# Cross-attention, gated MLP and squared-ReLU MLP on one core: other places for early loads, weight stores and attention steps

## The chip, the core and the metric

One core of one Trainium2 chip runs the whole program in one launch. The metric is the device time of one execution in microseconds (us); the kernel before takes 1464.22 us, the median of three runs (1463.28 to 1471.02).

## What is computed

The reference is three layers, one after the other. Inputs are x (8 batches, 8 heads, 512 tokens, 64 values) and state (8, 8, 32, 64), float32; the MLP weights are float64.

```
scores  = x @ state^T / 8        a  = softmax(scores)    xread = a  @ state
scores2 = state @ x^T / 8        a2 = softmax(scores2)   sread = a2 @ x
t = concat(xread, sread) as (8 * 544 tokens, 512)
t = (sigmoid(t @ w_gate) * (t @ w_val)) @ w_out          # d_ff = 1536
t = relu(t @ w_in)^2 @ w_out2                            # d_ff = 2048
```

The result has 4352 x 512 float32 values.

## The kernel before

Every product is three TensorE matmuls: each float32 operand is split into a high and a low part, and `mm3` (lines 182 to 185) adds high x high, high x low and low x high in PSUM. So nearly all matmul rows carry one of the lines L183, L184, L185. A float64 weight block is first made float32 by `to_single` (lines 109 to 134: two ScalarE passes L116 and L118, four VectorE ones L119, L123, L127, L131) and then split (L138 on ScalarE, L139 on VectorE).

Since `a @ state` is followed at once by `@ w_gate` and `@ w_val`, the kernel multiplies the states by the weights first. The 1536 columns are six **chunks** of 256 gate and 256 value columns. `chunk_steps` loads the four weight blocks of a chunk, converts them (`conv_gv`), multiplies them with the states of four batches (`state_weights`, PSUM tile `ps_g`, copied out by L531 and L535 into `go`), and stores the products in DRAM (`store_g`, L543, tensors `gd`). The two `w_out` blocks of the chunk are converted on the way. The chunks run once for batches 0 to 3 and once for batches 4 to 7; for the second pass the converted weights are read back from `wd` in DRAM, where `state_weights` (L525) or `store_kept` (L511) has put them. Six weight blocks (`KEPT`) lie in buffers that are free until later output weights need them, so their store can wait; the others lie in a pool of two buffers (`wr_p`).

Attention of a batch has steps in two halves (`group_stages`): token-major x is loaded (`xtok`), transposed on TensorE (L318) and split (L324, L325), multiplied with a block-diagonal state (`ps_s`, L337), and goes through transpose, maximum, subtraction, exponential, sum, reciprocal, product and transpose on VectorE and ScalarE (L347 to L370) into the tile `a`. There is one block-diagonal tile, filled by GpSimd (`prep_diag`), and one buffer each for most temporaries. The softmax in the other direction comes much later; its token-major x is loaded by `load_xn` into one buffer.

A **unit** is one batch and 128 of the 1536 columns. Its front (`front_x`) loads the products `gd` of its batch and chunk into `gi` (L597), splits them into `gg` (L607 on ScalarE, L608 on GpSimd), multiplies them with `a` into `psg` and `psv`, takes the sigmoid of `psg` (L622), the product with `psv` (L630, VectorE) and splits it (L190, L191). Its back (`back1`) multiplies with `w_out` into four accumulators `acc`. There are twelve units for a batch. The first four batches run their units 0 to 5, then all four their units 6 to 11; the accumulators of a first segment are stored (`pd`) and added later.

Order: `spread` gives every step of chunks and attentions a place in units, and the units call these steps in turn. On top of this a scheduler sets the final order of each engine from its own estimate of times. Unless `issue_after` ties an instruction to another, it may move a load far ahead. `reads` is the list of the units' `gi` loads, and `behind(reads)` ties to its last one.

All loads and stores named here are issued by SyncE (SP) in order; an issue whose buffer is not free holds everything behind it.

Of the kernel before, what the change touches and what calls it, by code (L numbers as in the profile page):

```python
# [18 lines left out]
P = 128  # L19
# [3 lines left out]
QB = 4  # L23
# [9 lines left out]
def kernel(  # L33
# [12 lines left out]
    nc = tc.nc  # L46
    B, H, S, D = x.shape
    NS = state.shape[2]
# [4 lines left out]
    NF1 = DF1 // P  # L53
# [7 lines left out]
    BM = B // NM  # L61
# [33 lines left out]
    def helper(busy):  # L95

        return nc.gpsimd if busy else nc.vector
# [38 lines left out]
    def convert(raw, w, busy):  # L136
        cf = to_single(raw, busy)
        nc.scalar.copy(out=w[:, 0, :], in_=cf)  # L138
        helper(busy).tensor_sub(out=w[:, 1, :], in0=cf, in1=w[:, 0, :].bitcast(F32))  # L139
# [3 lines left out]
    def row_src(w, f):  # L143
        return [(every, w.bitcast(U32)[f * P : (f + 1) * P, :])]
# [16 lines left out]
    def width(b):  # L161
# [6 lines left out]
    w_dram = {  # L168
        (ch, c): dram.tile([P, 2, 512], F32, name=f"wd{ch}_{c}")
        for ch in range(NCH) for c in range(NPAIR)  # L170
    }
# [10 lines left out]
    def mm3(ps, lh, ll, rh, rl, start, stop, more=False):  # L182
        nc.tensor.matmul(ps, lh, rh, start=start, stop=False, skip_group_check=more)  # L183
        nc.tensor.matmul(ps, lh, rl, start=False, stop=False, skip_group_check=more)  # L184
        nc.tensor.matmul(ps, ll, rh, start=False, stop=stop, skip_group_check=more)  # L185
# [21 lines left out]
    diag = once_p.tile([P, 2, NPAIR, P], F32R, name="diag")  # L207
    nc.gpsimd.memset(diag.bitcast(U32), 0)

    def load_states(m):  # L210
        raw = f_p.tile([P, DM], F32, tag="xs", name="sraw", bufs=1)
        for i in range(BM):
            nc.sync.dma_start(
                out=raw[NS * i : NS * (i + 1)].rearrange("n (h d) -> n h d", h=H),
                in_=state[BM * m + i].rearrange("h n d -> n h d"),
            )
        return raw

    def prep_states(raw):
# [26 lines left out]
    by_pair = x.rearrange("b (g j k) s d -> b g j k s d", g=2, j=2)  # L246
# [24 lines left out]
    def load_xn(b, g):  # L271

        t = xn_p.tile([P, 2, 2 * NT, D], F32, tag="xn", name="xn")
        for j in range(2):
            nc.sync.dma_start(
                out=t[:, j],
                in_=by_pair[b, g, j].rearrange("c (t p) d -> p (c t) d", p=P),
            )
        loaded_xn[b, g] = t

    a_tiles = {}
# [213 lines left out]
    gv = {}  # L495
    g_out = {}

    reads, sigs = [], []

    def behind(done):  # L500
        return tc.issue_after(done[-1].ins) if done else nullcontext()

    KEPT = {key: NF1 // 2 + i for i, key in enumerate(
        ((1, 0), (1, 1), (1, 2), (1, 3), (2, 0), (2, 1))
    )}
    kept = []

    def store_kept(after):
# [4 lines left out]
    def conv_gv(ch, c, raw):  # L513
        if (ch, c) in KEPT:
            f = KEPT[ch, c]
            w1[f] = gv[ch, c] = w1_p.tile([P, 2, 512], F32R, name=f"o{f}")
            kept.append((w1[f], w_dram[ch, c]))
        else:
            gv[ch, c] = wr_p.tile([P, 2, 512], F32R, tag="w", name="w")
        convert(raw, gv[ch, c], False)  # L520

    def state_weights(ch, c, m):
        w = gv.pop((ch, c))
        if m == (ch < ONCE) and (m or (ch, c) not in KEPT):
            nc.sync.dma_start(out=w_dram[ch, c], in_=w.bitcast(F32))  # L525
        ps = [at_p.tile([P, 512], F32, tag="at", name="ps_g") for j in range(2)]
        for j in range(2):
            sh, sl = (st_t[:, i, c, j, :] for i in range(2))
            mm3(ps[j], sh, sl, w[:, 0, :], w[:, 1, :], True, True)
        o = go_p.tile([P, 2, 512], F32, tag="go", name="go")  # L530
        nc.scalar.copy(out=o[:, 0, :], in_=ps[0])  # L531
        if m:
            nc.vector.tensor_copy(o[:, 1, :], ps[1])
        else:
            nc.scalar.copy(out=o[:, 1, :], in_=ps[1])  # L535
        g_out[ch, c, m] = o
# [8 lines left out]
    def conv_out1(f, raw):  # L545
        if f not in w1:
            w1[f] = w1_p.tile([P, 2, 512], F32R, name=f"o{f}")
        convert(raw, w1[f], False)

    ONCE, PACED = 1, (3,)  # L550

    def chunk_steps(ch, m, outs):

        raws = {}
        jobs = [("p", c) for c in range(NPAIR)] + [("o", f) for f in outs]
        steps = []
        ready = m and ch >= ONCE

        def load(n):
            k, i = jobs[n]  # L560
            if ready:
                gv[ch, i] = raw_p.tile([P, 2, 512], F32R, tag="raw", name="wagain")
                nc.sync.dma_start(out=gv[ch, i].bitcast(F32), in_=w_dram[ch, i])
                return
            with behind(reads if ch in PACED and not m else ()):
                raws[n] = load_pair(ch, i) if k == "p" else load_raw(row_src(w_out1, i))

        def conv(n):
            k, i = jobs[n]
            with behind(sigs if ch in PACED and not m else ()):  # L570
                if k == "p":
                    conv_gv(ch, i, raws.pop(n))
                else:
                    conv_out1(i, raws.pop(n))

        steps += [lambda: load(0), lambda: load(1)]
        for n in range(len(jobs) + 2):
            if n < len(jobs):
                if not ready:
                    steps.append(lambda n=n: conv(n))  # L580
                if not ready and n + 2 < len(jobs):
                    steps.append(lambda n=n: load(n + 2))
            if 1 <= n <= NPAIR:
                steps.append(lambda n=n: state_weights(ch, n - 1, m))
                if ready and n + 1 < len(jobs):
                    steps.append(lambda n=n: load(n + 1))
            if 2 <= n <= NPAIR + 1:
                steps.append(lambda n=n: store_g(ch, n - 2, m))
        return steps
# [628 lines left out]
        hl = st["g"]  # L1218
        squared("s", ps.rearrange("p i n -> p (i n)"), raw=True, into=(hl[:, 0], hl[:, 1]))

    HALF = NF1 // 2
    segments = [(b, 0, HALF) for b in range(QB)] + [(b, HALF, NF1) for b in range(QB)]
    segments += [(b, 0, NF1) for b in range(QB, B + 1)]
    units = [(b, f, lo, hi - 1) for b, lo, hi in segments for f in range(lo, hi)]
    at_unit = {(b, f): i for i, (b, f, _, _) in enumerate(units)}
# [4 lines left out]
    def spread(fns, start, end):  # L1230

        for i, fn in enumerate(fns):
            queue.append((STEPS * (start + (end - start) * i / max(len(fns), 1)), len(queue), fn))
# [6 lines left out]
    raw = load_states(0)  # L1240
    att_a, att_b = {}, {}
# [18 lines left out]

    outs = {ch: list(range(FC * ch, FC * (ch + 1))) for ch in range(NCH)}
    spread(chunk_steps(1, 0, outs[1]), 0, 1)
    spread(chunk_steps(2, 0, outs[2]), 1.2, 3)
    spread(att_a[1], 1, 4)
    spread(att_a[2], 4, 8)
    spread(att_a[3], 8, 12)
    for ch in range(3, NCH):
        spread(chunk_steps(ch, 0, outs[ch]), 6 + 4.5 * (ch - 3), 10.5 + 4.5 * (ch - 3))
    second = []
    spread([lambda: second.append(load_states(1))], 21.5, 21.5)  # L1270
    spread([lambda: prep_states(second.pop())], 23.5, 23.5)
# [27 lines left out]
    for i, (b, f, lo, hi) in enumerate(units):  # L1299
        ch, ff = divmod(f, FC)  # L1300
# [20 lines left out]
    for i, (b, f, lo, hi) in enumerate(units):  # L1321
        count[0] = STEPS * i
        g = (front_x if b < B else front_s)(b, f)
# [97 lines left out]
```

## Time and profile before

| what | value |
|---|---|
| median of three runs | 1464.22 us |
| the profiled execution's own time | 1464.19 us |
| its span, first to last instruction | 1462.4 us |
| mean granted TensorE clock | 0.988 |
| TensorE busy | 1408.3 us, 96% |
| VectorE busy | 1029.2 us, 70% |
| ScalarE busy | 903.5 us, 62% |

The span is 1.8 us shorter than the execution's own time, and that time is 0.03 us from the median. Shares of the whole span hide that the start is another regime: in the first 50 us TensorE is busy for 30.30 us, between 200 and 250 us for all 50.

### The profile page before, as it was taken

How to read it: one execution, taken by the hardware profiler on the slowest of the kernel's cores; microseconds unless marked ns; L12 is line 12 of the kernel's file. 1: busy time of each engine (PE TensorE's matmuls, PEld its weight loads, DVE VectorE, ACT ScalarE, POOL GpSimd, SP SyncE). 2: the span in 40 equal slices, each digit the busy share in tenths (PEclk: the TensorE clock that was granted, in tenths of full speed). 3: DMA queues.
4: the chain of work that ended last, by engine and by line, in shares of the span. 5: the costliest groups of instructions: out<-in, count | busy, mean ns of one | idle time of the engine just before them, and what ended most of it. 6: DMA issues, size and time to landing. Idle time of an engine off the chain costs nothing.

```text
span 1462.4 us, 21778 instructions
## 1 busy us (share of the span) xinstructions
PE 1408.3 (96%) x7416; PEld 1201.1 (82%) x7416; DVE 1029.2 (70%) x1644; ACT 903.5 (62%) x1630; POOL 303.5 (21%) x280
## 2 busy tenths in 40 slices
PE   5889999999999899999999999999999999999998
PEld 3568788887777687888897888799989999988898
DVE  6969887578788878777426756756787578745665
ACT  6869786466668867675427744655667456655432
POOL 1112213223334443445004443100000000000000
PEclk9899999999999999999999999999999999999999
DMA  9879899799998573564858965765667566866765
GB/s 257 260 236 322 230 305 328 222 337 322 329 310 252 166 186 112 158 211 153 305 195 311 333 220 192 236 221 191 194 218 262 182 196 197 272 228 216 234 228 173
DMA packets 293119, 347.50 MB, mean 238 GB/s; under 512 B 108048, under 2 KB 204816, under 8 KB 293008
## 3 DMA queue, kind: packets, MB, share of 16 engines
q1 hardware_dynamic: 288112, 336.93, 71.7%
q0 software_dynamic: 2048, 7.34, 1.4%
q10 hardware_dynamic: 2848, 1.84, 0.4%
q8 instruction: 59, 0.97, 0.3%
q14 instruction: 52, 0.43, 0.1%
HBM read 248.51 MB, written 97.52 MB: 237 GB/s over the span
## 4 chain that ended last, share of the span: by engine, by line
PE 71%; DMA 9%; DVE 7%; ACT 6%; issue 3%; POOL 2%; SPq 1%; ACTq 0%; POOLq 0%; DVEq 0%
PE o L185 7%; PE o L183 7%; PE o L184 7%; PE acc L184 4%; PE acc L185 4%; PE acc L183 4%; PE px L183 3%; PE px L184 3%; PE px L185 3%; PE psg L183 3%; PE psv L183 2%; PE psg L184 2%; PE psg L185 2%; PE psv L184 2%; PE psv L185 2%
## 5 line engine op out<-in xcount | busy, mean ns | idle before, releaser
L608 POOL TENSOR_TENSOR gg<-gi,gg 128x512 fp32r<-128x512 f32 x96 | 132.6, 1382 | 311.7 <-ACT gg L607 281.3
L183 PE MATMUL o<-wp,gh 128*128 128x256 f32 x672 | 188.9, 283 | 1.9 <-DMA wp<-wt 1.8
L184 PE MATMUL o<-wp,gh 128*128 128x256 f32 x672 | 188.9, 283 | 0.0
L185 PE MATMUL o<-wp,gl 128*128 128x256 f32 x672 | 185.5, 283 | 0.0
L184 PE MATMUL acc<-gl,o 128*128 128x512 f32 (+1 forms) x432 | 163.4, 381 | 3.0 <-DVE gl L191 3.0
L185 PE MATMUL acc<-gh,o 128*128 128x512 f32 (+1 forms) x432 | 162.5, 379 | 0.0
L183 PE MATMUL acc<-gh,o 128*128 128x512 f32 (+1 forms) x432 | 137.4, 380 | 0.4 <-DVE yp L694 0.4
L183 PEld LDWEIGHTS o<-wp,gh 128*128 128x128 f32 x672 | 128.4, 191 | 5.6 <-ACT gh L1062 1.8
L184 PEld LDWEIGHTS o<-wp,gh 128*128 128x128 f32 x672 | 128.5, 191 | 2.6
L185 PEld LDWEIGHTS o<-wp,gl 128*128 128x128 f32 x672 | 126.6, 191 | 1.2
L1123 DVE TENSOR_TENSOR y<-o,y 128x512 f32<-128x512 f32 x144 | 97.0, 685 | 34.7 <-PE o L185 33.8
L191 DVE TENSOR_TENSOR gl<-g,gh 128x512 fp32r<-128x512 f32 (+1 forms) x108 | 86.0, 797 | 28.7 <-ACT gh L190 28.3
L183 PE MATMUL px<-xh,wi 128*128 128x512 f32 x256 | 100.8, 395 | 3.4 <-DVE c L1013 2.4
L184 PE MATMUL px<-xl,wi 128*128 128x512 f32 x256 | 100.6, 393 | 0.0
L185 PE MATMUL px<-xh,wi 128*128 128x512 f32 x256 | 99.8, 390 | 0.0
L184 PEld LDWEIGHTS acc<-gl,o 128*128 128x128 f32 x432 | 81.3, 188 | 20.3 <-DVE gl L191 6.0
L185 PEld LDWEIGHTS acc<-gh,o 128*128 128x128 f32 x432 | 81.4, 188 | 14.8
L183 PEld LDWEIGHTS acc<-gh,o 128*128 128x128 f32 x432 | 79.2, 188 | 16.3 <-ACT c L118 0.8
L190 ACT CAST gh<-g 128x512 fp32r<-128x512 f32 (+1 forms) x108 | 64.4, 596 | 44.7 <-DVE g L630 31.3
L183 PE MATMUL psg<-a,gg 128*128 128x512 f32 x192 | 77.6, 404 | 9.9 <-ACT sg L622 6.4
L630 DVE TENSOR_TENSOR g<-psv,sg 128x512 f32<-128x512 f32 x96 | 65.4, 681 | 30.3 <-PE psv L185 21.0
L1053 ACT ACTIVATE c<-c 128x512 f32<-128x512 f32 x72 | 45.4, 631 | 65.5 <-DVE c L1013 64.8
(222 smaller groups left out, 3820.8 us busy)
## 6 DMA issues: line engine op xcount, KB each, us to landing
wi<-wi SPq DMA_DIRECT2D x256, 256.0 KB, 3.8
gd<-go SPq DMA_DIRECT2D x192, 128.0 KB, 4.2
gi<-gd SPq DMA_DIRECT2D x96, 256.0 KB, 4.1
wp<-wt SPq DMA_DIRECT2D x96, 256.0 KB, 3.5
wp<-wo SPq DMA_DIRECT2D x72, 256.0 KB, 3.5
wi<-wa SPq DMA_DIRECT2D x32, 512.0 KB, 4.6
wo<-wo SPq DMA_DIRECT2D x32, 512.0 KB, 4.8
ws<-wd SPq DMA_DIRECT2D x24, 512.0 KB, 5.8
```

Of the source, the lines that this page charges most:

```text
L183: nc.tensor.matmul(ps, lh, rh, start=start, stop=False, skip_group_check=more)
L184: nc.tensor.matmul(ps, lh, rl, start=False, stop=False, skip_group_check=more)
L185: nc.tensor.matmul(ps, ll, rh, start=False, stop=stop, skip_group_check=more)
L190: nc.scalar.copy(out=gh[:, :n], in_=g32[:, :n])
L191: nc.vector.tensor_sub(out=gl[:, :n], in0=g32[:, :n], in1=gh[:, :n].bitcast(F32))
L608: nc.gpsimd.tensor_sub(out=t[:, 1], in0=src, in1=t[:, 0].bitcast(F32))
L630: nc.vector.tensor_mul(out=g32, in0=ps, in1=sg)
L1053: nc.scalar.activation(out=r, in_=c, func=AF.Relu)
L1123: nc.vector.tensor_add(out=y, in0=ps[to, j], in1=y)
```

## The change

Five things differ. `load_states` and `load_xn` are tied behind the first `gi` load: for the states of batches 4 to 7 and for the first `xn` this decides; the first state load has no read to wait for and stays. Two more weight blocks, (2, 2) and (2, 3), are stored behind a `gi` load, ahead of the six kept ones; they lie in the pool of two buffers. The first segments of batches 0 and 1 have four units and not six, so the order of units is batch 0 (0 to 3), batch 1 (0 to 3), batch 2 (0 to 5), batch 3 (0 to 5), and then the rest. Chunk 2 is spread over units 2 to 5 (it was 1.2 to 3), the attentions of batches 1, 2, 3 over 1 to 2.6, 2.6 to 5, 5 to 8.5 (they were 1 to 4, 4 to 8, 8 to 12), and the chunks from the third on over 4.2 units each from 8 (they were 4.5 each from 6).

```diff
     def load_states(m):
         raw = f_p.tile([P, DM], F32, tag="xs", name="sraw", bufs=1)
         for i in range(BM):
-            nc.sync.dma_start(
+            with behind(reads[:1]):
+                nc.sync.dma_start(
...
         for j in range(2):
-            nc.sync.dma_start(
-                out=t[:, j],
+            with behind(reads[:1]):
+                nc.sync.dma_start(
+                    out=t[:, j],
...
+    LAST = ((2, 2), (2, 3))
...
             gv[ch, c] = wr_p.tile([P, 2, 512], F32R, tag="w", name="w")
+            if (ch, c) in LAST:
+                kept.insert(LAST.index((ch, c)), (gv[ch, c], w_dram[ch, c]))
...
-        if m == (ch < ONCE) and (m or (ch, c) not in KEPT):
+        if m == (ch < ONCE) and (m or (ch, c) not in (*KEPT, *LAST)):
...
-    HALF = NF1 // 2
-    segments = [(b, 0, HALF) for b in range(QB)] + [(b, HALF, NF1) for b in range(QB)]
+    FIRST = (4, 4, 6, 6)
+    segments = [(b, 0, FIRST[b]) for b in range(QB)] + [(b, FIRST[b], NF1) for b in range(QB)]
...
-    spread(chunk_steps(2, 0, outs[2]), 1.2, 3)
-    spread(att_a[1], 1, 4)
+    spread(chunk_steps(2, 0, outs[2]), 2, 5)
+    spread(att_a[1], 1, 2.6)
```

The names in the order: `xn` is token-major x for the later softmax, `sraw` the raw states, `raw` a float64 weight block; `gd_2_124` is the product of chunk 2 for batch 0, `gd_0_128` that of chunk 0 for batch 1. On SyncE, at the very start, before:

```order
L156 DMA raw<-in_moe_w_val_dram 128x2x256
L275 DMA xn<-in_x_dram 128x8x64 x2
L213 DMA sraw<-in_state_dram 32x8x64 x4
L156 DMA raw<-in_moe_w_gate_dram 128x2x256
L156 DMA raw<-in_moe_w_val_dram 128x2x256
L106 DMA raw<-in_moe_w_out_dram 128x1024
```

On SyncE, at the first unit's read, now:

```order
L602 DMA gi<-gd_0_122 128x2x256 x2
L219 DMA sraw<-in_state_dram 32x8x64
L548 DMA gd_1_123<-go 32x2x512
L548 DMA gd_1_129<-go 32x2x512
L548 DMA gd_1_135<-go 32x2x512
L548 DMA gd_1_141<-go 32x2x512
L156 DMA raw<-in_moe_w_gate_dram 128x2x256
```

The six issues have left the first weight loads and stand between the stores of chunk 1 and the loads of chunk 2 (the other three `sraw` and the two `xn` follow a dozen rows on). On SyncE, the read of the fifth unit, before (batch 0, chunk 2):

```order
L348 DMA sd_0_196<-s_900 128x512
L543 DMA gd_2_124<-go 32x2x512
L543 DMA gd_2_130<-go 32x2x512
L543 DMA gd_2_136<-go 32x2x512
L543 DMA gd_2_142<-go 32x2x512
L597 DMA gi<-gd_2_124 128x2x256 x2
```

and now (batch 1, chunk 0):

```order
L355 DMA sd_0_196<-s_781 128x512
L271 DMA xtok<-in_x_dram 128x8x64 x2
L602 DMA gi<-gd_0_128 128x2x256
L355 DMA sd_1_197<-s_851 128x512
L602 DMA gi<-gd_0_128 128x2x256
L514 DMA wd_2_180<-w 128x1024
L548 DMA gd_2_124<-go 32x2x512
```

The fifth unit now reads a product that was stored long ago, and the store of chunk 2 comes behind it. On ScalarE, the products of chunk 3 (`go` copies), before, among the sigmoids of several units:

```order
L622 ACTIVATE sg<-psg 128x512
L531 COPY go<-ps_g 128x512
L116 ACTIVATE q<-raw 128x512
L535 COPY go<-ps_g 128x512
L351 ACT_TABLE_LOAD
L351 ACTIVATE e_1383<-e_1383 128x512
L607 CAST gg<-gi 128x512
L138 CAST w<-c 128x512
L190 CAST gh<-g_1516 128x512
```

and now, the last of a block that lies between the sigmoids of the fourteenth and the fifteenth unit:

```order
L138 CAST w<-c 128x512
L536 COPY go<-ps_g 128x512
L138 CAST o_540<-c 128x512
L116 ACTIVATE q<-raw 128x512
L540 COPY go<-ps_g 128x512
L376 CAST a<-a_1436 128x512
L118 ACTIVATE c<-raw 128x512
L536 COPY go<-ps_g 128x512
L118 ACTIVATE c<-raw 128x512
L540 COPY go<-ps_g 128x512
L627 ACT_TABLE_LOAD
L627 ACTIVATE sg<-psg 128x512
```

All eight `go` copies of chunk 3 now stand between two sigmoids, together with the last part of the attention of batch 3.

## Rows read from the trace of the kernel before

**Rows 1.** First line of the page: busy time, share, instructions.

```profile
PE 1408.3 (96%) x7416; PEld 1201.1 (82%) x7416; DVE 1029.2 (70%) x1644; ACT 903.5 (62%) x1630; POOL 303.5 (21%) x280
```

**Rows 2.** Stretches: length, busy PE, PEld, DVE, ACT, POOL, clock, DMA share, GB/s.

```profile
0.00:50.00 50.00, 30.30 (x80) 19.06 (x81) 38.24 (x78) 36.19 (x63) 9.06 (x18) 0.83 1.00 276
70.00:80.00 10.00, 10.00 (x49) 8.31 (x48) 9.22 (x18) 7.34 (x14) 0.00 (x0) 1.00 0.65 196
80.00:90.00 10.00, 7.81 (x36) 5.43 (x34) 4.34 (x8) 5.81 (x9) 1.16 (x4) 1.00 0.55 148
90.00:100.00 10.00, 8.11 (x28) 6.43 (x29) 7.04 (x12) 5.96 (x8) 2.52 (x2) 0.66 1.01 333
200.00:250.00 50.00, 50.00 (x222) 40.85 (x221) 39.57 (x66) 35.20 (x64) 14.78 (x13) 1.00 0.97 332
```

**Rows 3.** Timeline of ScalarE: sigmoids of units 4, 5, 6, 10, 14, 22.

```profile
73.37 0.59 ACT L622 ACTIVATE sg<-psg 128x512 f32<-128x512 f32 x1
...
95.70 0.60 ACT L622 ACTIVATE sg<-psg 128x512 f32<-128x512 f32 x1 [1.15 <-PE psg L185]
...
102.05 0.60 ACT L622 ACTIVATE sg<-psg 128x512 f32<-128x512 f32 x1
...
126.18 0.59 ACT L622 ACTIVATE sg<-psg 128x512 f32<-128x512 f32 x1
...
158.21 0.58 ACT L622 ACTIVATE sg<-psg 128x512 f32<-128x512 f32 x1
...
214.65 0.60 ACT L622 ACTIVATE sg<-psg 128x512 f32<-128x512 f32 x1
```

**Rows 4.** Timeline of TensorE: the fifth unit's start, and a dense stretch.

```profile
91.89 0.79 PE L183 MATMUL psg<-a,gg 128*128 128x512 f32 x1 [3.28 <-ACT gg L607]
...
92.90 0.63 PE L183 MATMUL psv<-a,gg 128*128 128x512 f32 x1
93.33 0.63 PE L184 MATMUL psv<-a,gg 128*128 128x512 f32 x1
...
209.79 0.39 PE L183 MATMUL psg<-a,gg 128*128 128x512 f32 x1
...
211.61 0.39 PE L185 MATMUL psv<-a,gg 128*128 128x512 f32 x1
```

**Rows 5.** Chain that ended last, the piece ahead of the fifth unit.

```profile
88.38 2.76 DMA gi<-gd
```

**Rows 6.** Timeline of VectorE around the fourth unit's product.

```profile
70.16 0.42 DVE L119 TENSOR_SCALAR c<-c 128x512 f32<-128x512 f32 x1
70.49 0.69 DVE L131 CUSTOM_DVE_ANT_0 c<-c,q 128x1024 uint16<-128x1024 uint16 x1
...
74.77 0.68 DVE L630 TENSOR_TENSOR g<-psv,sg 128x512 f32<-128x512 f32 x1
75.37 0.68 DVE L139 TENSOR_TENSOR o<-c,o 128x512 fp32r<-128x512 f32 x1
```

**Rows 7.** Timeline of ScalarE: an operation after a sigmoid, and a table load.

```profile
73.86 0.61 ACT L138 CAST o<-c 128x512 fp32r<-128x512 f32 x1
...
100.75 1.28 ACT L622 ACT_TABLE_LOAD   x1
```

**Rows 8.** Timeline of SyncE, at the start.

```profile
7.16 1.49 SPq L275 DMA_DIRECT2D xn<-in_x_dram  x2
8.77 3.93 SPq L213 DMA_DIRECT2D sraw<-in_state_dram  x4
12.80 0.39 SPq L156 DMA_DIRECT2D raw<-in_moe_w_gate_dram  x1
```

**Rows 9.** Waits of the first 60 us: total, times, longest.

```profile
DVE q L127 <- DMA raw<-in_moe_w_val_dram: 8.5, 1, 8.5
```

**Rows 10.** Timelines of GpSimd and VectorE at one moment.

```profile
63.27 2.83 POOL L608 TENSOR_TENSOR gg<-gi,gg 128x512 fp32r<-128x512 f32 x2 [12.07 <-ACT gg L607]
...
63.43 1.52 DVE L119 TENSOR_SCALAR c<-c 128x512 f32<-128x512 f32 x1
```

More of the change, by code (lines that the diff above doesn't have):

```diff
@@ L208, with behind @@
     nc.gpsimd.memset(diag.bitcast(U32), 0)
+    reads, sigs = [], []
+    def behind(done):
+        return tc.issue_after(done[-1].ins) if done else nullcontext()
     def load_states(m):
@@ L212, in load_states @@
         for i in range(BM):
-            nc.sync.dma_start(
-                out=raw[NS * i : NS * (i + 1)].rearrange("n (h d) -> n h d", h=H),
-                in_=state[BM * m + i].rearrange("h n d -> n h d"),
-            )
+            with behind(reads[:1]):
+                nc.sync.dma_start(
+                    out=raw[NS * i : NS * (i + 1)].rearrange("n (h d) -> n h d", h=H),
+                    in_=state[BM * m + i].rearrange("h n d -> n h d"),
+                )
         return raw
@@ L274, in load_xn @@
         for j in range(2):
-            nc.sync.dma_start(
-                out=t[:, j],
-                in_=by_pair[b, g, j].rearrange("c (t p) d -> p (c t) d", p=P),
-            )
+            with behind(reads[:1]):
+                nc.sync.dma_start(
+                    out=t[:, j],
+                    in_=by_pair[b, g, j].rearrange("c (t p) d -> p (c t) d", p=P),
+                )
         loaded_xn[b, g] = t
@@ L496 @@
     g_out = {}
-    reads, sigs = [], []
-    def behind(done):
-        return tc.issue_after(done[-1].ins) if done else nullcontext()
     KEPT = {key: NF1 // 2 + i for i, key in enumerate(
@@ L1262 @@
     spread(chunk_steps(1, 0, outs[1]), 0, 1)
-    spread(chunk_steps(2, 0, outs[2]), 1.2, 3)
-    spread(att_a[1], 1, 4)
-    spread(att_a[2], 4, 8)
-    spread(att_a[3], 8, 12)
+    spread(chunk_steps(2, 0, outs[2]), 2, 5)
+    spread(att_a[1], 1, 2.6)
+    spread(att_a[2], 2.6, 5)
+    spread(att_a[3], 5, 8.5)
     for ch in range(3, NCH):
-        spread(chunk_steps(ch, 0, outs[ch]), 6 + 4.5 * (ch - 3), 10.5 + 4.5 * (ch - 3))
+        spread(chunk_steps(ch, 0, outs[ch]), 8 + 4.2 * (ch - 3), 12.2 + 4.2 * (ch - 3))
     second = []
```

## The prediction

> **What bounds the kernel now.** I read the page first. TensorE is busy for 1408.3 of 1462.4 us [rows 1], so at most 54 us of idle time can go, and the question is where it lies. The stretches answer that: TensorE has 30.30 busy us in the first 50, and from 200 to 250 us all 50 [rows 2]. The change reorders work ahead of the 22nd unit and hardly behind it, so only the first 215 us count.
>
> A busy TensorE can be a slow one, so I measured lateness. In a dense stretch matmuls start 0.2275 us apart (the last of rows 4 starts 1.82 us and eight matmuls behind the one above it); between 92 and 97 us they start 0.43 us apart, and the granted clock of 90 to 100 us is 0.66, so this is partly the lower of the two clock levels [rows 2, 4]. I counted, in the order, the 512-wide matmuls up to the last `psg` of a unit (four transposes as one), took 0.2275 us for each, and subtracted that from the time of the unit's sigmoid [rows 3]. What is left is the time that TensorE has lost so far:
>
> - unit 4: 73.37 - 140 x 0.2275 = 41.5
> - unit 5: 95.70 - 208 x 0.2275 = 48.4
> - unit 6: 102.05 - 218 x 0.2275 = 52.5
> - unit 10: 126.18 - 323 x 0.2275 = 52.7
> - unit 14: 158.21 - 456 x 0.2275 = 54.5
> - unit 22: 214.65 - 690 x 0.2275 = 57.7
>
> So 41.5 us are lost before the fourth unit, where weights are converted; 11.0 between the fourth and the sixth; 5.2 in small pieces up to the 22nd. The 11.0 are one jam: the fifth unit is the first that needs chunk 2, and TensorE stands 3.28 us for its `gg` [rows 4], because its load stands in SyncE's order directly behind the stores of chunk 2 and takes 2.76 us of the chain [rows 5]. Then the clock is low for some 12 matmuls, 12 x 0.2 = 2.4 us.
>
> At the 22nd unit both orders have 690 matmuls behind them, so the change in lateness there is the change in time: up to 250 us TensorE has no idle time behind it [rows 2], and little is moved there.
>
> **The change part by part.** *The loads behind the first read.* Two `xn` and four `sraw` issues, 1.49 and 3.93 us of SyncE, leave the front of the fourth weight load, which went out at 12.80 us [rows 8]. At most these 5.4 us could come back. But in the first 60 us VectorE waited for weights only once, up to 8.5 us [rows 9], and these loads were issued ahead of the moved ones. I take 0. Put back behind the first read they are 768 KB among the loads of chunk 2: at the 276 GB/s of the first 50 us [rows 2] that is 768 x 1024 / 276,000 = 2.8 us of a DMA system whose share is already 1.00. Queued behind them are chunk 2's weights, and behind these ScalarE and VectorE in order. Cover: chunk 2 is now first needed by the 13th unit. I take 0, and keep 2.8 for the range.
>
> *The two stores behind later reads.* They held two buffers that chunk 3 needs. Each moves behind a read between the fifth and the tenth unit; the next writer of these buffers now runs around the 14th. 0 from both sides.
>
> *Up to the fourth unit.* The order now has more attention work there. On VectorE I counted 66 long operations ahead of the fourth unit's product and not 56, 53 short ones and not 52, 7 reductions over 512 and not 4 (a few tiny ones left out). A long one takes 0.60 us from start to start, a short one 0.33 [rows 6], a reduction as a long one: 13 x 0.60 + 0.33 = 8.1 us. VectorE is nearly without gaps ahead of the fourth unit (9.22 us busy from 70 to 80 us [rows 2]), so I add all of it: the product comes at 74.77 + 8.1 = 82.9 us. TensorE has 153 matmuls ahead and not 140, 3.0 us more, so lateness grows by 5.1, to 46.6.
>
> *Unit 4 to unit 6.* The jam goes: unit 5 now reads chunk 0 of batch 1. It needs batch 1's `a` instead. Between the fourth and fifth unit TensorE has 60 matmuls, 13.7 us; VectorE has 17 long and reduction operations and one short, 17 x 0.60 + 0.33 = 10.5 us. So TensorE leads, and the attention chain that runs beside it (exponential, table loads of 1.28 us [rows 7]) can add something. Bounds: 0, and the 11.0 that this stretch cost before. I take 2.0, near the lower end, because TensorE has 3 us more work than VectorE: 48.6 at the sixth unit, against 52.5.
>
> *Unit 6 to unit 14.* At the tenth unit both orders have 192 VectorE operations behind them, but ScalarE two more table loads, 2.6 us, partly beside other work. I take 1.5 for these and 1.0 for small waits: 51.1 at the 14th, against 54.5.
>
> *Unit 14 to unit 15.* Here now stand all of chunk 3's products and the end of batch 3's attention. TensorE has 70 matmuls, 15.9 us (before: 16); ScalarE 23 operations at 0.49 us [rows 3, 7] and two table loads, 13.8 us; VectorE 17 long and reduction and 7 short ones, 12.5 us. They depend on each other in turns: two weight buffers, two PSUM buffers. Three engines with nearly equal work and no slack wait for each other: bounds 0 and again 11.0. I take 4.0, the remaining units as before at 0: 55.1 at the 22nd, against 57.7.
>
> The sum: -3.9 up to the sixth unit (5.1 lost, 9.0 won), +0.5 to the 14th, +0.8 to the 22nd (4.0, where before it was 3.2), so 57.7 - 55.1 = 2.6 us won. Against the profiled execution's own 1464.19 us, which is the median within 0.03 us, that is 1461.6; I say 1461.5.
>
> *A rule against the change.* While GpSimd ran two `gg` subtractions, a short VectorE operation took 1.52 us where 0.42 is usual [rows 6, 10]. The Trainium skill (GPSIMD Engine Reference, 1. Specifications) says that GpSimd's SBUF interfaces are shared with VectorE and that the two contend when VectorE runs in a two-port mode or has two SBUF inputs. The rule agrees with that row. By it, GpSimd work brought into the stretch where VectorE is the bound is paid for by VectorE: the diagonal tile of batch 3 is filled ahead of the ninth unit's `gg` and not of the eleventh's, and if one VectorE operation more is stretched by 1.1 us, the sum would be -1.5 and not -2.6. I stay with the sum.
>
> **The rivals.**
>
> *The jam goes and none takes its place.* For it: between 60 and 90 us DMA is little used (0.55 from 80 to 90, [rows 2]) and VectorE is idle for more than half of 80 to 90 us, and the new order fills just this. Against it: the fuller block at unit 15. Price: lateness stays at 46.6 to 50, so 7.7 to 11.1 are won: 1453 to 1456.5, and 1452 with a little of the start.
>
> *Slower: the block ahead of the fifteenth unit becomes the jam.* Its 24 state matmuls stand in TensorE's order ahead of the unit's front, the third weight block must wait until the first has left its buffer, and ScalarE, with 13.8 us of work, must do its part in between, while batch 3's `a` waits in the same queue. If it costs 11.0, as the jam before, lateness is 62.1, 4.4 worse: 1468.6; with the low clock behind it and small waits, up to 1472. It decides from 6.6 us of lost time there: then the whole gain is gone. For it: near-equal work on three engines. Against it: nothing there goes to DRAM and back.
>
> *Slower: the moved loads delay chunk 2's weights.* VectorE and ScalarE take chunk 2's conversions between the first units' steps, in order, so a late weight block holds the units. 2.8 us and a dropped clock: 1465 to 1469. For it: a DMA share of 1.00. Against it: the loads are issued some 10 us ahead of use.
>
> *The change does not do what it says.* The order shows the issues where the title says, so I give it nothing.
>
> **How the numbers follow.** Forecast (1457 to 1465): 0.50. Jam gone: 0.25. Block at unit 15: 0.17. Late weights: 0.08. Less than 0.5%, 7.3 us, cannot be told from no change by a measurement of this kernel: below 1456.9 is faster, above 1471.5 slower. Faster: the jam-gone case, 0.25. Slower: the upper part of the two slower cases and what several such waits together would add, 0.15. Same: 0.60. The range reaches into both sides, 1452 to 1472; the forecast's own range is 1457 to 1465.
>
> **What would show it.** Each by the time and place in the profile after: the fourth unit's product near 83 us and not 75 (up to the fourth unit); no idle time of TensorE over 2 us ahead of the fifth unit, and no `gi` load in the chain there (the jam); the sixth sigmoid near 100 us (48.6 + 224 x 0.2275 = 99.6); ScalarE and TensorE alternating between the 14th and 15th sigmoid, which then lie about 20 us apart (15.9 + 4.0); the 22nd sigmoid near 212 us. If the fourth unit's product is as early as before, or the 22nd sigmoid is under 207 or over 220 us, a step is wrong. A difference that arises behind the 22nd unit would refute the claim that only the start matters.

## The result: slower by 1.5%, where a gain of 0.2% was forecast

The kernel after takes 1486.58 us (median of six runs, 1484.95 to 1488.64), the kernel before 1466.01 (six runs, 1463.28 to 1471.02). The ratio is 1.0147, 95% interval 1.0127 to 1.0166, so some 21 us are lost. The forecast was 1461.5 us, its range 1452 to 1472.

The profiled execution after took 1485.15 us, with a span of 1483.4 us and a mean granted clock of 0.989 (before 0.988). First line of the page after, which answers to [rows 1]:

```profile
PE 1411.9 (95%) x7416; PEld 1199.0 (81%) x7416; DVE 1036.7 (70%) x1644; ACT 903.1 (61%) x1630; POOL 308.7 (21%) x280
```

The instruction counts are the same. TensorE is busy only 3.6 us longer than in [rows 1], so most of the 21 us is time in which it stands idle. Where? The stretches after (length, busy PE, PEld, DVE, ACT, POOL, clock, DMA share, GB/s); the first five answer to [rows 2]:

```profile
0.00:50.00 50.00, 27.36 (x80) 17.38 (x80) 36.66 (x73) 34.42 (x59) 9.68 (x18) 0.90 0.91 262
70.00:80.00 10.00, 6.49 (x28) 4.85 (x28) 8.25 (x16) 8.68 (x14) 4.49 (x6) 0.99 0.56 169
80.00:90.00 10.00, 9.85 (x39) 8.04 (x40) 9.53 (x15) 8.84 (x16) 3.05 (x2) 0.84 0.68 183
90.00:100.00 10.00, 8.95 (x41) 6.79 (x40) 8.06 (x15) 6.57 (x12) 0.00 (x0) 1.00 0.99 310
200.00:250.00 50.00, 50.00 (x224) 41.44 (x223) 44.05 (x74) 38.72 (x70) 11.24 (x11) 1.00 1.02 363
250.00:300.00 50.00, 46.88 (x203) 37.48 (x203) 26.02 (x40) 22.08 (x39) 15.06 (x14) 1.00 0.82 264
500.00:550.00 50.00, 43.76 (x199) 35.47 (x198) 40.94 (x65) 35.35 (x69) 20.41 (x17) 0.97 0.59 159
```

The same two last stretches of the kernel before:

```profile
250.00:300.00 50.00, 50.00 (x221) 41.20 (x220) 27.10 (x42) 22.28 (x39) 13.10 (x11) 1.00 0.78 254
500.00:550.00 50.00, 46.73 (x222) 38.37 (x221) 38.34 (x61) 36.09 (x73) 20.87 (x17) 1.00 0.63 165
```

At 200 to 250 us TensorE is as busy as before. In the next 50 us it runs 203 matmuls where it ran 221, at the same clock. So most of the loss lies behind the part that the prediction worked out. The sigmoids after, of units 4, 5, 6, 14, 15, 22, which answer to [rows 3]:

```profile
83.12 0.60 ACT L627 ACTIVATE sg<-psg 128x512 f32<-128x512 f32 x1
...
99.18 0.60 ACT L627 ACTIVATE sg<-psg 128x512 f32<-128x512 f32 x1
...
104.53 0.60 ACT L627 ACTIVATE sg<-psg 128x512 f32<-128x512 f32 x1
...
153.26 0.59 ACT L627 ACTIVATE sg<-psg 128x512 f32<-128x512 f32 x1
...
172.86 0.60 ACT L627 ACTIVATE sg<-psg 128x512 f32<-128x512 f32 x1
...
218.22 0.60 ACT L627 ACTIVATE sg<-psg 128x512 f32<-128x512 f32 x1
```

The lateness below is the prediction's measure, with matmuls counted in the traces; that gives one matmul more, 0.2 or 0.3 us less lateness, than the prediction has for before (52.2, 54.2 and 57.4 us at units 6, 14 and 22). The difference to before is +3.6 at the 22nd unit, +4.6 as a mean over units 25 to 30, +12.1 over units 46 to 51, +22.3 over units 73 to 84, and then stays. So nearly 18 of 22.3 us arise between the 30th and the 73rd unit.

What waits there? The longest waits of TensorE between the 30th and the 73rd sigmoid, before (total, times, longest):

```profile
PE ps_sr L437 <- DVE et L416: 3.8, 2, 2.5
PE acc L184 <- DVE gl L191: 3.0, 4, 1.4
PE psg L183 <- ACT sg L622: 2.8, 3, 1.2
```

and after:

```profile
PE acc L184 <- DVE gl L191: 6.2, 6, 2.9
PE psv L183 <- DVE g L635: 4.1, 4, 1.4
PE psg L183 <- ACT sg L627: 3.5, 2, 2.8
PE acc L183 <- ACT gh L190: 3.5, 2, 2.4
```

TensorE waits for the units' own small steps on VectorE and ScalarE. All its waits in this stretch come to 10.4 us before and 20.4 after, so they make some 10 of the nearly 18 us. The same stretch as a whole, before and then after:

```profile
263.64:561.78 298.14, 287.64 (x1294) 233.81 (x1293) 233.83 (x371) 202.47 (x364) 112.93 (x99) 1.00 0.83 260
271.72:582.04 310.32, 289.55 (x1281) 232.47 (x1280) 232.89 (x363) 199.34 (x360) 115.21 (x99) 0.99 0.79 244
```

The granted clock is 1.00 before and 0.99 after. Twice after (458.8 to 462.0 and 527.1 to 530.3 us) it is at 0.50, the lower level of 1.2 GHz, and both times TensorE had waited shortly before, 2.84 us up to 457.57 and 2.36 us up to 525.27. By the clock's share this is another 3 us (an estimate, 0.01 x 310.32). The rest is no more than a lateness is uncertain by (some 4 us, see the table below).

The steps that TensorE waits for are short. In the longest case the step is late because something ahead of it in the queue waits. The longest wait after, on VectorE:

```profile
283.48 0.46 DVE L127 TENSOR_SCALAR q<-raw 128x512 uint16<-128x512 uint16 x1 [8.74 <-DMA raw<-in_moe_w_in_dram]
283.83 0.68 DVE L635 TENSOR_TENSOR g<-psv,sg 128x512 f32<-128x512 f32 x1
```

A unit's product stands directly behind a weight conversion that waited 8.74 us for its block. TensorE feels little of this: it waits 1.02 us for the product,

```profile
284.56 0.50 PE L183 MATMUL psv<-a,gg 128*128 128x512 f32 x1 [1.02 <-DVE g L635]
```

and 0.91 us for the step behind it, some 2 of the 20.4 us. The piece of the chain of waits ahead of it, after:

```profile
267.68 4.59 DMA yd<-yp
...
272.33 0.32 SPq L712
...
272.77 3.96 DMA yd<-yp
...
276.74 0.32 SPq L712
...
277.15 6.30 DMA raw<-in_moe_w_in_dram
```

On SyncE the loads of partial sums (`yp`, L712) stand ahead of the weight block, and two of them wait 4.59 and 3.96 us for a buffer to be stored (`yd`). Before, that order on SyncE is the other way round, the weight block ahead of the `yp` load:

```profile
274.83 1.13 SPq L702 DMA_DIRECT2D yd<-yp  x2
276.01 0.46 SPq L106 DMA_DIRECT2D raw<-in_moe_w_in_dram  x1
276.56 0.80 SPq L597 DMA_DIRECT2D gi<-gd  x1
280.12 0.33 SPq L707 DMA_DIRECT2D yp<-pd  x1
```

From the 31st unit on both kernels run the same batches, blocks and places, and the scheduler orders the same work in another way. What it enters this part with is not the same: the change ends batch 0 with the 28th unit and not with the 30th. In the case traced here that end takes part, because the `yd` stores are batch 0's and the `yp` loads batch 1's; they come two units earlier, while the weight block kept its place.

### The profile page after: what moved, and what is told of

Read it like the earlier page. It is cut to its first block, busy times and chain, and to the rows that moved or that the text cites. A ratio compares the mean times of both kernels' runs of the same rounds, so it can differ in the third digit from the quotient of the medians.

```text
span 1483.4 us, 21781 instructions
## 1 busy us (share of the span) xinstructions
PE 1411.9 (95%) x7416; PEld 1199.0 (81%) x7416; DVE 1036.7 (70%) x1644; ACT 903.1 (61%) x1630; POOL 308.7 (21%) x280
## 4 chain that ended last, share of the span: by engine, by line
PE 71%; DVE 9%; ACT 7%; DMA 6%; issue 4%; POOL 1%; SPq 1%; ACTq 0%; DVEq 0%; POOLq 0%
PE o L185 7%; PE o L183 7%; PE o L184 7%; PE acc L184 4%; PE acc L185 4%; PE acc L183 4%; PE px L183 3%; PE px L184 3%; PE px L185 3%; PE psg L183 2%; PE psg L184 2%; PE psg L185 2%; PE psv L183 2%; PE psv L184 2%; PE psv L185 2%
## 5 line engine op out<-in xcount | busy, mean ns | idle before, releaser
L613 POOL TENSOR_TENSOR gg<-gi,gg 128x512 fp32r<-128x512 f32 x96 | 137.4, 1432 | 341.1 <-ACT gg L612 303.9
L191 DVE TENSOR_TENSOR gl<-g,gh 128x512 fp32r<-128x512 f32 (+1 forms) x108 | 89.1, 825 | 26.8 <-ACT gh L190 26.2
L183 PE MATMUL psg<-a,gg 128*128 128x512 f32 x192 | 78.1, 407 | 15.5 <-ACT sg L627 10.4
```

The costliest lines, as they stand in the source:

```text
L191: nc.vector.tensor_sub(out=gl[:, :n], in0=g32[:, :n], in1=gh[:, :n].bitcast(F32))
L613: nc.gpsimd.tensor_sub(out=t[:, 1], in0=src, in1=t[:, 0].bitcast(F32))
```

## The experiments

All ratios are to the kernel before, run on the same chip, with 95% intervals.

The table has the difference in lateness to before (us, from the sigmoids of one profiled execution each; a row is uncertain by some 4 us, as e7 and e14 show, whose times are those of before, so growths that differ by less than that are not told apart). "Growth" is the last column of lateness less the one of units 25 to 30.

```
run              unit 4  13-15  25-30  73-84  growth  time ratio
ScalarE and VectorE in the order of before, units 37 to 72:
e2_stores          -1.9   -1.5    0.6    1.2     0.7  1.0008
e14_states          3.7    1.7    4.1    5.0     1.0  0.9985
e7_spreads         -1.5   -1.1    3.0    4.0     1.1  0.9991
e4_loads_stores     4.7    2.9    9.9   11.2     1.3  1.0047
e15_before_later    0.4   -0.9   -0.6    0.9     1.5  0.9987
e8_loads_gg         4.3    1.3    7.1    9.0     1.9  1.0031
e1_loads            4.1    1.4    8.5   12.3     3.8  1.0044
e13_xn              4.7    1.6    6.4   11.3     4.9  1.0036
another order there:
e5_nudge            0.7    1.2    3.2    5.9     2.7  1.0028
e11_full_nudge      9.0    2.0    6.2   10.1     3.9  1.0055
e16_plan_nudge     -1.3   -3.5   -0.1    7.5     7.6  1.0030
e9_before_early    -1.6   -1.7   -0.4    9.7    10.0  1.0059
e3_plan            -0.4   -3.2    0.1   11.1    11.0  1.0057
e12_plan_late       0.0   -4.2   -1.2   13.1    14.3  1.0060
e10_full_late       6.8    0.3    5.1   21.7    16.7  1.0120
e6_first           -1.8    7.0   21.7   38.6    17.0  1.0259
the change          6.8    0.7    4.6   22.3    17.8  1.0147
```

### The parts by themselves

**e1_loads**: the two ties of the loads alone.

```diff
+            with behind(reads[:1]):   # load_states, load_xn
...
```

> The kernel before with the two load ties alone (states and token-major x behind the first unit's read). Theory A (the loss comes from the order behind the 22nd unit, which only the new plan of segments and places changes much): within 6 us of before, since the order of ScalarE and VectorE is the same as before from about the 36th unit on. Theory B (the moved loads hold chunk 2's weights and all that follows): at least 8 us slower than before.

Measured: 1.0044 (1.0024 to 1.0064), 5.7 us: inside A's 6 and short of B's 8, but a loss, where the prediction put nothing. The first unit is 5.6 us late. ScalarE's cast of the first product waits at the head of its queue, since the scheduler now puts it ahead of two more weight conversions:

```profile
46.96 0.62 ACT L609 CAST gg<-gi 128x512 fp32r<-128x512 f32 x1 [6.09 <-DMA gi<-gd]
47.48 0.61 ACT L138 CAST o<-c 128x512 fp32r<-128x512 f32 x1
```

By the sixth unit this is gone (-0.2), because the old jam at the fifth unit takes it up. Then lateness grows again between units 17 and 27, to 8.6.

**e2_stores**: the two further stores behind later reads alone.

```diff
+    LAST = ((2, 2), (2, 3))
...
```

> The kernel before with the two weight stores behind later reads alone. Theory A: within 6 us of before; order the same from about the 36th unit on. Theory C (late stores hold the two-buffer pool and so chunk 3's conversion): at least 8 us slower, with the loss ahead of the 24th unit.

Measured: 1.0008 (0.9993 to 1.0024). The stores cost nothing, as forecast; C falls.

**e3_plan**: segments and places alone.

```diff
+    FIRST = (4, 4, 6, 6)
...
+    spread(chunk_steps(2, 0, outs[2]), 2, 5)
...
```

> The kernel before with first segments of 4, 4, 6, 6 units and the new places of chunks and attentions alone; loads and stores as before. Theory A: 12 to 22 us slower than before, most of it between the 22nd and the 60th unit, as in the changed kernel. Theories B and C: within 6 us of before.

Measured: 1.0057 (1.0037 to 1.0077), about 8 us (1473.75 against 1466.15): the place is A's, the size is not. Its lateness is 48.9 at the sixth unit, 50.5 at the 14th, 55.8 at the 22nd (before 52.2, 54.2, 57.4): the early gain is there. It is lost between units 31 and 67.

**e4_loads_stores**: e1 and e2 together.

> The kernel before with the load ties and the store change, old segments and places. Theory A: within 6 us of before. Theory B or C: 8 us slower or more. If the loss needs all edits together, this one is within 6 us and the plan alone is too.

Measured: 1.0047 (1.0033 to 1.0061), as e1. Loads (1.0044) and plan (1.0057) add to 1.010; the whole change has 1.0147, so some 7 us, uncertain by some 5, come only with both.

### Is the loss behind the 24th unit the plan's or the order's?

**e5_nudge**: before, with one neutral edit.

```diff
-        spread(chunk_steps(ch, 1, []), 24.5 + 4.5 * ch, 29 + 4.5 * ch)
+        spread(chunk_steps(ch, 1, []), 24.7 + 4.5 * ch, 29.2 + 4.5 * ch)
```

> The kernel before with one neutral edit: the second pass of the chunks (batches 4 to 7) is placed 0.2 of a unit later (24.7 and 29.2 in place of 24.5 and 29). Nothing of the change is in it; the instructions are the same, their order is that of before up to about the 24th unit and differs from there to the 96th. Theory P (the loss behind the 22nd unit comes from the moved ends of the first segments): within 3 us of before, lateness at units 64 and 94 within 2 us of 72.7 and 74.2. Theory O (whatever makes the scheduler arrange units 24 to 72 anew costs some microseconds, because small waits at the heads of ScalarE's and VectorE's queues come and go with the order): 4 to 12 us slower than before, with the lateness growing between the 31st and the 72nd unit.

Measured: 1.0028 (1.0015 to 1.0042), 3.8 us. A fifth of a unit, with nothing of the change in it, costs just under the 4 us that theory O gave as its least; P's bound of 3 us is just passed. Where the loss arises the lateness does not show: a growth of 2.7 us is within the uncertainty of a row.

**e6_first**: the segments alone.

```diff
+    FIRST = (4, 4, 6, 6)
...
```

> The kernel before with the segments alone: the first segments of batches 0 and 1 have four units, all places of chunks and attentions are those of before. The source from the 30th unit on is the same as before's, but the order differs up to about the 96th unit. Theory P (moved ends of segments): 8 to 15 us slower than before, all of it behind the 22nd unit. Theory O (order behind the 24th unit): 4 to 12 us slower, also behind the 22nd unit. Theory S (the loss of the plan comes from the new places of attentions and chunks): within 3 us of before. Up to the 22nd unit every theory expects a little gain or none, since the jam at the fifth unit goes.

Measured: 1.0259 (1.0231 to 1.0288), 36 us. No theory has that. Two losses: about 20 us between the 13th and the 16th sigmoid (+1.6 to +21.8), and 17 behind the 30th unit. The first lies where batch 3's `a` is first needed, at the 15th unit; with the old places it comes too late (14th and 15th sigmoid at 163.23 and 191.54 us; before 158.21 and 164.76). Between 140 and 200 us all waits of TensorE come to 12.0 us, and the granted clock is 0.90. The longest in the stretch 140 to 190 us:

```profile
PE psg L183 <- ACT a L369: 4.1, 1, 4.1
```

So the new places are needed by the new segments. The second loss is that of theories P and O alike.

**e7_spreads**: places of attentions and chunks alone (chunk 2 as before).

```diff
+    spread(att_a[1], 1, 2.6)   # and att_a[2], att_a[3], chunks from the third on
```

> The kernel before with the new places alone: attentions of batches 1, 2, 3 over units 1 to 2.6, 2.6 to 5, 5 to 8.5, chunks from the third on over 4.2 units each from 8; segments and chunk 2 as before. Its order is that of before again from the 36th unit on. Theory P and theory O both: within 4 us of before, and no growth of the difference between the 36th and the 72nd unit. Theory S (these places make the loss): 6 to 12 us slower, as the whole plan (8.3 us).

Measured: 0.9991 (0.9974 to 1.0009). No loss; theory S falls.

**e9_before_early**: before, with the last layer's weights converted one unit earlier.

```diff
-    spread(free, 30.6, PACE[0])
+    spread(free, 29.6, PACE[0])
```

> The kernel before with one edit: the conversions of the last layer's weights start one unit earlier (29.6 in place of 30.6). Up to the 24th unit the order is that of before. On VectorE it then stands as in the changed kernel: 42 weight conversions and 393 operations ahead of the 32nd unit's product (before 41 and 388, changed 42 and 396), 52 and 589 ahead of the 54th's (before 51 and 581, changed 53 and 591). Theory R (the changed kernel's loss behind the 30th unit comes from VectorE's and ScalarE's order running one weight conversion ahead, so that the units' work queues behind it and behind weights that have not landed): 8 to 15 us slower than before, lateness growing between units 30 and 60. Theory O (chance of the order): between 3 us faster and 6 us slower, as the nudge of 0.2 of a unit (4 us slower).

Measured: 1.0059 (1.0040 to 1.0079), 10 us, all between units 30 and 73. This fits R in size and is beyond O's 6.

**e10_full_late** and **e12_plan_late**: the changed kernel, and the plan alone, with these conversions from 33 on.

```diff
-    spread(free, 30.6, PACE[0])
+    spread(free, 33, PACE[0])
```

> The changed kernel with one edit: the same conversions start 2.4 units later (33). Up to the 24th unit its order is the changed kernel's; ahead of the 32nd unit's product stand 41 conversions and 389 operations again (before 41 and 388), ahead of the 54th's 52 and 583 (before 51 and 581). Theory R: most of the loss behind the 30th unit comes back, 8 to 15 us faster than the changed kernel, 1472 to 1479. Theory O: within 5 us of the changed kernel, 1482 to 1492.

> The segments and places alone, with the conversions of the last layer's weights from 33 on in place of 30.6. This keeps the gain of the plan up to the 22nd unit (1.6 to 3.7 us in the record of the plan alone). Theory R: the 11 us that the plan alone loses between units 31 and 67 fall to 3 or less, 1463 to 1467, as fast as before or a little faster. Theory O: 1468 to 1478, as the plan alone (1473.8).

Measured: 1.0120 (1.0100 to 1.0141) and 1.0060 (1.0032 to 1.0087): 1483.7 and 1475.7 us, as without the edit. VectorE no longer stands ahead, and the loss is there all the same. R had forecast that most of it comes back; both runs are against it, and within what O gave.

**e11_full_nudge**: the changed kernel with the nudge of e5.

> The changed kernel with the neutral nudge of before (second pass of the chunks 0.2 of a unit later). Up to the 24th unit the order is the changed kernel's; VectorE stands at 41 conversions and 390 operations ahead of the 32nd unit's product and at 51 and 580 ahead of the 54th's, as before's. Theory R: 5 to 12 us faster than the changed kernel, since the run ahead is gone by the way. Theory O: within 5 us of the changed kernel.

Measured: 1.0055 (1.0036 to 1.0074), 1473.9 us. A neutral fifth of a unit takes back 12.7 of the change's 20.6 us. O, with its 5 us, misses; R, with 5 to 12, is nearly met. But R's count is not the cause: e10 and e11 both have 41 conversions ahead of the 32nd unit's product, nearly the same number of operations, and lie 9.8 us apart. The start is as late as the changed kernel's (6.2 at units 25 to 30, against 4.6); the growth behind it is 3.9 and not 17.8. Waits of VectorE for the last layer's first weights, between the 30th and the 73rd sigmoid, in before, the change, and e11:

```profile
DVE q L127 <- DMA raw<-in_moe_w_in_dram: 7.5, 5, 3.3
```

```profile
DVE q L127 <- DMA raw<-in_moe_w_in_dram: 10.5, 3, 8.7
```

```profile
DVE q L127 <- DMA raw<-in_moe_w_in_dram: 18.0, 6, 5.2
```

e11 waits longest in sum and yet loses less than the change: the sum of such waits does not decide. That what stands behind a wait decides would fit this, and the row of the product at 283.83 us; it was not tested.

**e16_plan_nudge**: the plan alone with the nudge.

> The segments and places alone with the neutral nudge of the second pass (24.7 and 29.2). Up to the 24th unit it has the plan's order, from the 49th on that of the changed kernel with the nudge, which lost 3 to 4 us there (lateness 6.6 above before's at the 48th unit, 10.1 at the 72nd) where the plan lost 6.5 (4.6 and 11.1). Theory O: 3 to 4 us lost between the 48th and the 72nd unit here too, and in all 1466 to 1471, faster than the plan alone (1473.8) and the changed kernel. Theory P (the loss behind the 24th unit belongs to the moved segment ends): 1472 to 1476, as the plan alone.

Measured: 1.0030 (1.0011 to 1.0049), 1471.1 us. From the 49th unit on its order is row for row that of e11, though its start is some 6 us earlier. Between the 48th and the 72nd unit the difference to before grows by 2.8 us (4.5 to 7.3), in e11 by 3.5 (6.6 to 10.1), in the plan without the nudge by 6.5 (4.6 to 11.1). So the same order loses about the same from two starts, though 2.8, 3.5 and 6.5 us are hardly told apart. The time lies between what O gave (up to 1471) and what P gave (from 1472), so it decides neither way. What speaks against P as a fixed price of the moved segment ends is e11: they are in it, and its growth is 3.9 us.

### Is the loss of the moved loads their transfer?

**e8_loads_gg**: e1 with the first `gg` cast tied one conversion later (`made` lists the weight casts).

```diff
-    split_gw(0, 0)
...
+    with tc.issue_after(made[-1].ins):
+        split_gw(0, 0)
...
```

> The kernel with the two moved loads alone, and ScalarE's first cast of the first unit's product tied one weight conversion later (it stood 6.1 us at the head of ScalarE's queue, waiting for its load). Nothing else moves behind the first unit. Theory H (the loss of the moved loads comes from this wait at the head of the queue): the lateness of the first unit falls from 43.9 to 38 to 41, and the time to within 3 us of before. Theory L (the loss arises on its own between units 17 and 24, where TensorE, ScalarE and VectorE wait for weights; the first unit's wait is taken up by the jam at the fifth): the first unit is earlier all the same, but by the sixth the lateness is that of before and of the loads alone (52), and the time stays 4 to 8 us above before.

Measured: 1.0031 (1.0014 to 1.0048), which e1's interval overlaps. The wait was only shortened, from 6.09 to 4.13 us, and the first unit's lateness fell to 41.3. By the sixth unit it is that of before (-0.5), and between units 17 and 27 it grows to 7.2 as in e1. H allowed 3 us and L gave 4 to 8; by the medians it is 3.7 us, between the two, but the place is L's.

**e13_xn**, **e14_states**: each load's tie alone.

> The kernel before with the token-major x load alone tied behind the first unit's read (two issues, 512 KB). Its order in units 13 to 24 is nearly that of the kernel with both loads tied and not that of before; from the 37th unit on it is before's. Theory O (the order makes the loss): 4 to 8 us slower, as both loads, with the lateness growing between units 17 and 24. Theory T (the transfers among chunk 2's weights make it, by their bytes): also slower, about two thirds of both loads' 5.7 us, but the loss ahead of the 13th unit.

> The kernel before with the load of the second group's states alone tied (four issues, 256 KB). Its order in units 13 to 24 is close to before's (about nine rows in ten), from the 25th unit on it is before's. Theory O: within 3 us of before. Theory T: about a third of both loads' 5.7 us, some 2 us slower, ahead of the 13th unit.

Measured: 1.0036 (1.0018 to 1.0053) for `xn`, 0.9985 (0.9965 to 1.0005) for the states. So the loss of the loads is that of `xn`. Its transfer is issued at 47.64 us, but the loss arises between 200 and 230 us, where it has long landed:

```profile
208.35 0.62 ACT L608 CAST gg<-gi 128x512 fp32r<-128x512 f32 x1
211.55 0.62 ACT L138 CAST w<-c 128x512 fp32r<-128x512 f32 x1 [2.57 <-DMA wd<-w]
...
226.28 0.80 ACT L116 ACTIVATE q<-raw 128x512 uint16<-128x512 uint32 x1 [1.93 <-DMA raw<-in_moe_w_val_dram]
```

ScalarE stands at the head of its queue, once for the store of an older weight block whose buffer it needs, once for a block that has not landed. Before, the casts of that place (205.71 and 207.13 us) wait for no store. How much of the loss these two waits make is not shown: TensorE's own waits between 200 and 240 us come to 2.1 us here, and before it has none there.

**e15_before_later**: before with chunks from the third on half a unit later, so that the order of units 13 to 24 is disturbed as in e1, and no load is moved.

```diff
-        spread(chunk_steps(ch, 0, outs[ch]), 6 + 4.5 * (ch - 3), 10.5 + 4.5 * (ch - 3))
+        spread(chunk_steps(ch, 0, outs[ch]), 6.5 + 4.5 * (ch - 3), 11.0 + 4.5 * (ch - 3))
```

> The kernel before with no load moved: the chunks from the third on are placed half a unit later (6.5 in place of 6). Its order in units 13 to 24 differs from before's as much as that of the moved loads; from the 37th unit on it is before's. Theory O: it loses some microseconds between units 13 and 36, 2 to 8 us slower, nothing behind. Theory T: within 2 us of before.

Measured: 0.9987 (0.9970 to 1.0004). Here T is right and O, as I put it (2 to 8 us), misses: another order need not cost. Against T stands the place: e13 loses between units 17 and 27, and T put its loss ahead of the 13th, where e13 is at +1.6. So what remains is that this order of those units costs and another one, as far from before's, does not.

## Why the prediction was wrong

**The step that failed: "up to 250 us TensorE has no idle time behind it [rows 2], and little is moved there".** From this the prediction took the change at the 22nd unit as the change in time and put everything behind it at nothing. The first half holds after as well (50.00 of 50 us). The second was never looked at behind the 24th unit. There the order on ScalarE and VectorE agrees with before's in 0.3 to 0.7 of its rows up to the 72nd unit, and nearly 18 of the 22.3 us arise. The prediction named this as what would refute it. Up to the 22nd unit it missed too, by less: it had 2.6 us won there, and 3.6 were lost.

**The moved loads: "I take 0", at most 2.8 us lost.** They cost 5.7 us (e1). Nothing came back at the front: the gate block behind them (the fourth gate block, the seventh weight load) went out at 11.31 us and not at 12.80, but the one wait for weights, whose load goes out ahead of them in both kernels, is 8.3 us after where [rows 9] have 8.5:

```profile
DVE q L127 <- DMA raw<-in_moe_w_val_dram: 8.3, 1, 8.3
```

For the transfer that I had priced no run shows a cost (e14; the place of e13's loss). But with the two `xn` issues out of SyncE's first 13 us the scheduler arranges units 1 to 24 anew. In the changed kernel, too, ScalarE's cast for the first unit stands at the head of its queue and waits for its load, which it did not before:

```profile
44.44 0.62 ACT L612 CAST gg<-gi 128x512 fp32r<-128x512 f32 x1 [3.39 <-DMA gi<-gd]
```

The first unit is 3.6 us late, and the loads have a part in the late fourth unit and in the +3.6 at the 22nd.

**Up to the fourth unit: +5.1, product at 82.9 us.** Its sigmoid is at 83.12 us, lateness +6.8; the product starts at 85.39, where [rows 6] have 74.77:

```profile
85.39 0.69 DVE L635 TENSOR_TENSOR g<-psv,sg 128x512 f32<-128x512 f32 x1 [0.20 <-PE psv L185]
```

The count of VectorE's work holds: ahead of this product VectorE is busy for 68.6 us, before for 60.2, 8.4 us more where 8.1 were counted. What was wrong is that it was put down to the attentions. With the plan alone VectorE has 62.9 busy us ahead of the product, which comes at 76.51 us, and the difference in lateness is -0.4; with the loads alone it is +4.1. The order with all this work ahead of the fourth unit arises only with both.

**The jam at the fifth unit goes: right.** Between 84 and 99.5 us no row of TensorE has idle time ahead of it. Still lateness rises by 5.2 us between the fourth and the sixth unit (48.1 to 53.3), where 2.0 were taken and before has 10.9. For the plan alone the forecast of lateness seems to hold: 48.6, 51.1 and 55.1 were forecast for units 6, 14 and 22, 48.9, 50.5 and 55.8 came out. At the sixth unit that is luck: two terms are off by nearly as much and cancel, 40.9 in place of 46.6 at the fourth unit, and 8.0 in place of 2.0 from there to the sixth. The changed kernel is 4.3 to 5.2 us above the plan alone, with the loads.

**Unit 14 to unit 15: 4.0 and 20 us apart.** 3.6 (54.8 to 58.4) and 19.6 us. ScalarE alternates with TensorE there as foretold:

```profile
155.24 0.58 ACT L536 COPY go<-ps_g 128x512 f32<-128x512 f32 x1
158.02 0.59 ACT L344 COPY s<-ps_s 128x512 f32<-128x512 f32 x1 [2.20 <-PE ps_s L185]
160.74 0.59 ACT L540 COPY go<-ps_g 128x512 f32<-128x512 f32 x1 [2.13 <-PE ps_g L185]
```

**The two stores: 0.** Right (e2).

**The rivals.** The jam at the 15th unit did not come; late weights of chunk 2 did not either, though their price, 1465 to 1469, is by chance near that of the loads. The case that happened, many small waits behind the 30th unit out of an order made anew, was none of them. On the rule against the change the traces say this: up to the 22nd unit 14 VectorE operations before and 15 after take over 0.4 us longer than the median of their kind, in sum 12.1 and 13.7 us, and GpSimd is busy beside every one of them (beside 68 of all 321 before). The rule on shared SBUF interfaces (the Trainium skill, GPSIMD Engine Reference, 1. Specifications) fits these rows. No run here isolates it, and what TensorE loses by it is not shown.

**What is shown and what is open.** Shown: eight kernels with the order of before in units 37 to 72 lose 0.7 to 4.9 us more behind the 30th unit, though they enter it between 0.6 us early and 9.9 late; nine with another order lose 2.7 to 17.8, so another order can cost much and need not; edits that only move later work a little, and with it the order there, change the changed kernel by -12.7 or -3 us and the kernel before by +3.8 or +10. One instance, some 2 us of TensorE's waits, is traced to its cause, the weight block behind two `yp` loads; moving it alone was not tried, and the longer waits of 2.84 and 2.88 us were not traced. Not excluded is that the moved segment ends make a costly order more likely: of the seven kernels that have them six grow by 7.6 us or more, of the two other orders without them one does (e9). Open: which property of an order decides. Neither the number of conversions that run ahead (e10, e11, e12) nor the sum of waits for weights (e11) does. How large the effect of an edit on the order would be was not foreseen either: O's figures missed in e6, e9, e11 and e15, and barely in e5. No version was faster than before by more than the measurement tells.

## What to carry to other kernels

Where a scheduler makes the final order from its own clock, an edit of the start is also an edit of everything behind it: compare the two orders to the end of the program before saying that only the start counts. Before crediting or blaming an edit, give each kernel one or two neutral nudges; here shifts of a fifth of a unit moved the time by -12.7 and +3.8 us and a shift of a whole unit by +10, while the early gain of the plan alone was 3.3 us at the sixth unit and 1.6 at the 22nd. Where an instruction waits for a transfer, look at the row that follows it in the queue, and then at what the busiest engine waits: here 8.74 us of VectorE were 2 us of TensorE.

## What was not expected of the hardware

Nothing in how an engine or a transfer behaves. The granted clock of the whole span is 0.988 before and 0.989 after and so does not show the loss. By place it takes part, as said above: between the 30th and the 73rd sigmoid it is 1.00 before and 0.99 after, some 3 us, behind waits of TensorE.
